# Phases of a gated recurrence as running sums of angles, with every step of the kernel in a new order

## The chip, the core and the metric

The kernel runs on one core of one Trainium2 chip. The core has five engines, each with its own in-order instruction queue: PE (TensorE, matrix products; its weight loads are listed as PEld), DVE (VectorE), ACT (ScalarE), POOL (GpSimd) and SP (SyncE, which here only issues DMAs). They synchronise through semaphores. Work waits for its inputs and for a free buffer, and everything queued behind a waiting instruction on the same engine waits too. The metric is the device time of one execution in microseconds; a kernel's time is the median of its runs.

## The reference

Inputs q, k, v, a_re, a_im have the shape (4, 8, 768, 48): batch, heads, tokens, channels. A complex gate per token and channel multiplies a state, then the rows of x go through a two-layer MLP.

```python
mag = np.sqrt(a_re * a_re + a_im * a_im)
scale = np.minimum(mag, 0.999) / (mag + 1e-06)
a_re_n, a_im_n = (a_re * scale, a_im * scale)
for t in range(S):
    ar, ai = (a_re_n[:, :, t, :, None], a_im_n[:, :, t, :, None])
    new_re = ar * S_re - ai * S_im
    new_im = ar * S_im + ai * S_re
    kv = np.einsum('bhd,bhe->bhde', k[:, :, t], v[:, :, t])
    S_re, S_im = (new_re + kv, new_im)
    y[:, :, t] = np.einsum('bhd,bhde->bhe', q[:, :, t], S_re)
...
h = x @ w_in
g = np.maximum(h, 0.0) + alpha * np.minimum(h, 0.0)
return (g @ w_out).astype(np.float32)
```

x is y with heads and channels side by side: 3072 tokens of 384. w_in is 384 x 2048, w_out 2048 x 384; both arrive as 64-bit floats.

A gate is a size times a rotation. So the state is real in a frame that turns: k and q are multiplied by the cosine and sine of the phase summed up so far, and only the sizes remain as decays.

## The kernel before, in words

**Units.** A unit is one chunk of 128 tokens of one batch, all 8 heads: 24 units, function `unit`. A unit turns q and k by the phases (L661, L663, tile PP), multiplies them by decays for block widths 1, 2, 4, 8, 16, 32 (`step`, L717; ACT copies at L740 and L756), forms products of queries and keys per block (`meet`, L678), masks them (L699 on ACT, L702 on DVE), transposes the keys (L785, L787), forms the new state (L797, L826, L829) and the result (L817, L841), which ACT copies out (L855) and two DMAs write to ysc (L860).

**Gates.** `gates` makes what the units load. It runs over nine groups, lettered A to I: batch 0 in groups of 1, 2 and 3 chunks, each other batch in two groups of 3. 384 head-channels lie as 3 x 128 rows, so a group of C chunks has N = 3 x 128 x C columns: 384, 768, and 1152 for a full group. The steps up to L310 normalise: ACT squares and takes reciprocal roots, DVE multiplies; `dec` holds the sizes, `x` and `y` the unit rotations. L318 multiplies sizes pairwise, level by level, and L323 writes them to the DRAM tensor decs, from which a unit loads T (L594). The phases are products of rotations: seven complex products within blocks of 8 tokens (`product`, L338 and L340), seven more over blocks of 64, one running chain over those (`run`, `carry`), a renormalisation (L405 to L413), and a last complex product per token (L426, L429). L431 writes cosine and sine to phs, from which a unit loads PP (L587). Operations of up to 80 elements go to POOL for batches 1 to 3 and to DVE for batch 0. The tile gate has two buffers, so group g's loads (L250) wait for group g - 2.

**Weights.** Sixteen pieces of 64-bit weights are loaded (L491) and converted to float32 by ACT (L507, L509, L511), POOL (L515) and DVE (L517, L519).

**MLP.** `features` multiplies a token group by one of 16 slices of w_in (L889, two PSUM buffers ps_h), ACT takes Relu (L896), DVE adds the rest (L898); `outputs` multiplies by w_out (L908), and L918 and L921 send it out. L873 loads x from ysc.

**The order.** Every piece of work is a Python generator; each `yield` ends a step that issues one to a few dozen instructions. The string ORDER names the generator that goes on next, a letter per step: A to I gates, J unit loads, K and L loads of v, M small loads and weights, N and O weight conversion, P to Z and a to m units 0 to 23, n the loads of x, o the MLP. The engines' queues are filled in this order and in no other; the numbers given to DVE(...), ACT(...) and the like at a yield are ignored here.

```python
for c in order:
    next(self.tasks[self.LETTERS.index(c)], None)
```

## Time and profile before

| what | value |
|---|---|
| median of 3 runs | 855.87 us (851.8 to 855.99) |
| span of the profiled execution | 853.8 us |
| mean granted TensorE clock | 0.958 |
| DMA traffic, mean | 130.91 MB, 153 GB/s |
| chain that ended last, by engine | PE 62%, DVE 17%, DMA 11%, issue 4%, ACT 3% |
| unit 0: first matmul, last result DMA | 50.6, 116.9 us |
| unit 3: first matmul, last result DMA | 173.6, 200.1 us |
| first load of x (L873) | 121.4 us |
| unit 23: last result DMA | 799.7 us |

A group of the profile's instruction list has its line, engine, operation, tiles written and read, shape and count, then busy time and the mean length of one in ns, then the idle time of its engine just before and what ended it. In the table of forty slices each digit is the busy share of 21 us in tenths. The sum of single durations on an engine can exceed its busy time a little, as neighbouring instructions overlap.

### The profile page before, as it was taken

How to read it: one execution, taken by the hardware profiler on the slowest of the kernel's cores; microseconds unless marked ns; L12 is line 12 of the kernel's file. 1: busy time of each engine (PE TensorE's matmuls, PEld its weight loads, DVE VectorE, ACT ScalarE, POOL GpSimd, SP SyncE). 2: the span in 40 equal slices, each digit the busy share in tenths (PEclk: the TensorE clock that was granted, in tenths of full speed). 3: DMA queues.
4: the chain of work that ended last, by engine and by line, in shares of the span. 5: the costliest groups of instructions: out<-in, count | busy, mean ns of one | idle time of the engine just before them, and what ended most of it. 6: DMA issues, size and time to landing. Idle time of an engine off the chain costs nothing.

```text
span 853.8 us, 26837 instructions
## 1 busy us (share of the span) xinstructions
PE 702.5 (82%) x11488; PEld 534.1 (63%) x11488; DVE 650.8 (76%) x1020; ACT 441.3 (52%) x937; POOL 203.3 (24%) x293
## 2 busy tenths in 40 slices
PE   0000428678999898999999799999999999999998
PEld 0000416557777676776677577777777777777776
DVE  5999989998998799778999686788896754643212
ACT  7848786565736444564567333456544333332211
POOL 6322142306526202440036400530006100000000
PEclk9999858689999999899999899999999999999999
DMA  6796784875398369747874479357654455421000
GB/s 202 235 245 211 219 226 137 246 188 142 98 275 182 77 159 242 187 112 182 222 202 105 129 195 206 96 144 192 151 174 100 135 132 133 108 51 35 20 28 10
DMA packets 194174, 130.91 MB, mean 153 GB/s; under 512 B 74120, under 2 KB 185864, under 8 KB 194056
## 3 DMA queue, kind: packets, MB, share of 16 engines
q1 hardware_dynamic: 194056, 129.20, 57.8%
q8 instruction: 90, 1.47, 0.7%
q14 instruction: 28, 0.23, 0.1%
HBM read 100.82 MB, written 35.71 MB: 160 GB/s over the span
## 4 chain that ended last, share of the span: by engine, by line
PE 62%; DVE 17%; DMA 11%; issue 4%; ACT 3%; SPq 2%; DVEq 0%; ACTq 0%
PE ps_o L908 24%; PE ps_h L889 23%; DVE KQ L717 4%; PE ps_lv L678 4%; PE ps_y L817 4%; DMA T<-decs 4%; PE ps_kv L797 3%; PE ps_y L841 2%; DVE gate L426 2%; PE ps_kt L785 2%; DMA PP<-phs 2%; DMA gate<-in_a_re_dram 1%; DVE gate L298 1%; DMA phs<-gate 1%; DVE gate L318 1%
## 5 line engine op out<-in xcount | busy, mean ns | idle before, releaser
L889 PE MATMUL ps_h<-xT,w_in_sb 128*128 128x256 f32 (+1 forms) x1344 | 305.3, 358 | 10.7 <-DMA xT<-ysc 8.2
L908 PE MATMUL ps_o<-w_out_sb,g_sb 128*128 128x384 f32 x768 | 293.8, 498 | 5.2 <-DVE g_sb L898 4.2
L889 PEld LDWEIGHTS ps_h<-xT,w_in_sb 128*128 128x128 f32 x1344 | 234.6, 194 | 82.9 <-DMA xT<-ysc 8.4
L898 DVE SCALAR_TENSOR_TENSOR g_sb<-g_sb,al,ps_h 128x256 f32<-128x256 f32 (+1 forms) x224 | 97.2, 436 | 116.9 <-ACT g_sb L896 116.5
L896 ACT ACTIVATE g_sb<-ps_h 128x256 f32<-128x256 f32 (+1 forms) x224 | 78.7, 352 | 204.3 <-PE ps_h L889 203.1
L717 DVE TENSOR_TENSOR KQ<-KQ,T 96x1024 f32<-96x1024 f32 x120 | 148.1, 1234 | 40.3 <-PE ps_lv L678 34.5
L908 PEld LDWEIGHTS ps_o<-w_out_sb,g_sb 128*128 128x128 f32 x768 | 139.4, 193 | 58.7 <-DVE g_sb L898 7.9
L678 PE MATMUL ps_lv<-WQ 96*32 96x32 f32 x2304 | 34.0, 202 | 78.7 <-DVE WQ L661 50.6
L678 PEld LDWEIGHTS ps_lv<-WQ 96*32 96x32 f32 x2304 | 26.1, 115 | 99.2 <-DVE WQ L661 50.6
L740 ACT COPY WQ<-KQ 96x1024 f32<-96x1024 f32 x48 | 50.0, 1042 | 27.0 <-DVE KQ L717 26.8
L515 POOL TENSOR_SCALAR top<-top 128x768 f32<-128x768 f32 x16 | 45.8, 2862 | 73.5 <-ACT top L507 62.8
L855 ACT COPY T<-ps_y 48x256 f32<-48x256 f32 x96 | 30.9, 364 | 51.6 <-PE ps_y L841 50.9
L817 PE MATMUL ps_y<-A,VL 64*48 64x64 f32 x2304 | 45.4, 232 | 14.4 <-issue 13.4
L338 POOL TENSOR_TENSOR gate<-gate 128x72 f32<-128x72 f32 x42 | 27.5, 654 | 118.1 <-ACT gate L368 115.3
L817 PEld LDWEIGHTS ps_y<-A,VL 64*48 64x48 f32 x2304 | 43.1, 133 | 15.4 <-issue 14.2
L338 DVE TENSOR_TENSOR gate<-gate 128x576 f32<-128x576 f32 (+5 forms) x84 | 47.9, 571 | 1.3
L699 ACT ACTIVATE A<-ps_lv,columns 128x64 f32<-128x64 f32 x144 | 36.9, 335 | 20.4 <-PE ps_lv L678 20.4
L756 ACT COPY W<-KQ 96x512 f32<-96x512 f32 x48 | 30.7, 639 | 30.0 <-DVE KQ L717 24.9
L426 DVE TENSOR_TENSOR gate<-gate 128x1152 f32<-128x1152 f32 (+2 forms) x36 | 43.4, 1231 | 2.1 <-POOL gate L411 2.0
L678 PE MATMUL ps_lv<-KQ,W 96*32 96x32 f32 x1536 | 24.3, 204 | 17.8 <-ACT W L756 15.8
L702 DVE TENSOR_TENSOR A<-ps_lv,mask 128x256 f32<-128x256 f32 x96 | 37.4, 411 | 0.0
L787 ACT COPY T<-ps_kt 128x384 f32<-128x384 f32 x48 | 23.1, 480 | 26.8 <-PE ps_kt L785 26.7
(106 smaller groups left out, 904.8 us busy)
## 6 DMA issues: line engine op xcount, KB each, us to landing
T<-decs SPq DMA_DIRECT2D x48, 384.0 KB
PP<-phs SPq DMA_DIRECT2D x24, 387.0 KB
KQ<-in_q_dram SPq DMA_DIRECT2D x48, 192.0 KB
decs<-gate SPq DMA_DIRECT2D x7, 1152.0 KB
phs<-gate SPq DMA_DIRECT2D x14, 576.0 KB
KQ<-in_k_dram SPq DMA_DIRECT2D x40, 192.0 KB
vsc<-in_v_dram SPq DMA_DIRECT2D x48, 144.0 KB
VL<-vsc SPq DMA_DIRECT2D x24, 288.0 KB
```

Source lines behind the costliest of these rows:

```text
L338: on(4 * k).tensor_tensor(out=m, in0=w[:, 1::-1].unsqueeze(2).to_broadcast([P, 2, 2, k]), in1=pairs_of(u), op=ALU.mult)
L426: TT(out=m[:, a], in0=U5[:, 1 + a], in1=turned(off3, o)[:, a].unsqueeze(1).unsqueeze(3).to_broadcast([P, L // 2, nb, 2]), op=ALU.mult)
L515: nc.gpsimd.tensor_scalar(out=top, in0=top, scalar1=F64_SMALL, scalar2=None, op0=ALU.max)
L678: nc.tensor.matmul(t[64 * i + j:64 * i + j + HC // 2, p], lhsT=keys(n, g), rhs=queries(n, g), start=True, stop=True)
L702: nc.vector.tensor_tensor(out=a.rearrange("p n (g t) -> p n g t", g=2), in0=t.unsqueeze(2).to_broadcast(whole), in1=masks[name].rearrange( ...
L717: nc.vector.tensor_tensor(out=x, in0=x if x0 is None else x0, in1=m, op=ALU.mult)
L740: nc.scalar.copy(z.rearrange("p i n t -> p i (n t)").rearrange("p i (m h) -> p m i h", h=h), bass.AP(tensor=KQ.tensor, offset=KQ.offset + ...
L817: nc.tensor.matmul(o, lhsT=Vp[h][64 * i:64 * i + 64, s, e_ * D:(e_ + 1) * D], rhs=a, start=False, stop=False)
L889: nc.tensor.matmul(p, lhsT=w_in_sb[:, f // 2, kk, f % 2 * P:(f % 2 + 1) * P], rhs=x_of[m][:, kk], start=(kk == 0), stop=(kk == NK - 1))
L896: nc.scalar.activation(gt, p, AF.Relu, scale=-1.0)
L898: nc.vector.scalar_tensor_tensor(out=gt, in0=gt, scalar=al_1[:, f:f + 1], in1=p, op0=ALU.mult, op1=ALU.add)
L908: nc.tensor.matmul(sums[0], lhsT=gt[:, c * P:(c + 1) * P], rhs=w_out_sb[:, f], start=(f == 0), stop=(f == NF - 1))
```

## The change

The gates are computed another way, and ORDER is a new string of 3791 letters (4292 before). Per group:

- An angle per token: ACT and DVE form a reciprocal of the real part (Abs_reciprocal_sqrt, two Squares, two products as a correction), the quotient of imaginary and real part, and its Arctan.
- The phase is the running sum of the angles, three `tensor_tensor_scan` of n tokens, begun with the phase of the group before (`carry`). It is brought into one turn: an Identity adds 1.5 x 2^23, the low 16 bits are the number of whole turns, and DVE subtracts them.
- Sine and cosine come from Sin, the cosine through the absolute value of the phase; two DMAs write them to phs, now with the first column.
- The size is the sum of real part times cosine and imaginary part times sine of the token's own angle. It is clipped, divided through and multiplied pairwise as before, then written to decs, now after phs.
- Two steps of the form `tensor_scalar` run on POOL, in group A on DVE. A Sin of one column stands ahead of each Arctan.
- The complex products, their tiles and their small DMAs are gone. A group has 42 steps (41 where it is a batch's last) in place of 91 to 100. The units, loads, weights and MLP have the same steps as before, issued in the new order.

```diff
 ORDER = (
-    "AAAAAAAAAMJBMMMMMAAAAAAAAAOAAAAAKAAAABAAAAAAAAAKAAKAKKKKKKKKKAAOAKBOKOBOBJAANBNAABBBNAAAOAAAAAANNAMA"
-    "AAAAKNANABNNAAAANBAAAAABJBBBANABMBMABAOAONJOABAAABBBBBMBAAAABAAOBAABAABBBBKOBBBBBBBBBNNNNNBBJNBBPBBN"
...
-    "oooooooooooooooooooooooooooooooooooooooooooooooooooooooooooooooooooooooooooooooooooooooooooo")
+    "MMAJMMAAAAAAAAAANAAAAAAMBJNAAAAANJJMAAAABKLAALAMLNBAKKAAAAAANNABBBBAAAABBBONOOBOOOOOBBONNJKKKAKPNNPP"
+    "BBMJCJJCNBBBBBNNOBNBBBBBPPPPPNNPOOPJMMLBLKJBJMLCBKBBBNPBCBBBCPOOCPBBBBBBOOCCCCPCPPPOOPNNNNMCNNCCONJQ"
...
+    "ooooooooooooooooooooooooooooooooooooooooooooooooooooooooooooooooooooooooooooooooooooooooooo")
...
-    bias_half = next(column)
-    nc.vector.memset(bias_half, -0.5)
+    bias_round = next(column)
+    nc.vector.memset(bias_round, 1.5 * 2.0 ** 23)
+    bias_back = next(column)
+    nc.vector.memset(bias_back, -TURN / 4)
+    bias_quarter = next(column)
+    nc.vector.memset(bias_quarter, TURN / 4)
+    ones, trig = next(column), next(column)
+    nc.vector.memset(ones, 1.0)
...
-        flat = work.tile([P, 6 * NK * GT], F32, tag="gate", name="gate", bufs=2)[:, 0:6 * N]
-        G = flat.rearrange("p (r n) -> p r n", r=6)
-        x, c, f, d, e, y = [G[:, i] for i in range(6)]
-        dec = flat[:, 3 * N:5 * N].rearrange("p (m s) -> p m s", s=TL)
-        for z, src in ((x, a_re), (y, a_im)):
-            z = z.rearrange("p (t s) -> p t s", t=NK)
+        flat = work.tile([P, 6 * NK * GT + 2 * NK], F32, tag="gate", name="gate", bufs=2)
+        x, c, d, e = [flat[:, i * N:(i + 1) * N] for i in range(4)]
+        dec = flat[:, 2 * N:4 * N].rearrange("p (m s) -> p m s", s=TL)
+        wide = [flat[:, 4 * N + i * NK * (n + 1):4 * N + (i + 1) * NK * (n + 1)] for i in range(2)]
+        turn, sine = [z.rearrange("p (t s) -> p t s", t=NK) for z in wide]
+        spun, y = turn[:, :, 1:n + 1], sine[:, :, 1:n + 1]
+        def rows3(z):
+            return z.rearrange("p (t s) -> p t s", t=NK)
+        for z, src in ((rows3(x), a_re), (y, a_im)):
             rows = src[b].rearrange("n i d s -> (n i d) s").rearrange("(t p) s -> p t s", p=P)
             t = yield DMA(N / 2, ("gates", g - 2))
             if last:
                 nc.gpsimd.memset(z[:, :, n - 1:n], 0.0)
             nc.sync.dma_start(z[:, :, 0:n - last], rows[:, :, c0 * P + 1:c1 * P + 1 - last])
+            if z is y:
+                ty = t
+            else:
+                tx = t
+        if g:
+            t = yield POOL(N, tx)
+        else:
+            t = yield DVE(N // 2, tx)
+        (nc.gpsimd if g else nc.vector).tensor_scalar(out=d, in0=x, scalar1=1.5, scalar2=TINY, op0=ALU.mult, op1=ALU.add)
         t = yield ACT(N, t)
-        nc.scalar.activation(x, x, AF.Identity, scale=1.5, bias=bias_tiny)
-        yield ACT(N)
-        nc.scalar.activation(c, x, AF.Square, scale=GATE_SCALE)
+        nc.scalar.activation(c, d, AF.Abs_reciprocal_sqrt, scale=GATE_SCALE)
         t = yield ACT(N, t)
-        nc.scalar.activation(d, y, AF.Square, scale=1.5 * GATE_SCALE)
+        nc.scalar.activation(c, c, AF.Square)
+        t = yield ACT(N, t)
+        nc.scalar.activation(c, c, AF.Square)
         t = yield DVE(N, t)
-        TT(out=c, in0=c, in1=d, op=ALU.add)
+        TT(out=c, in0=d, in1=c, op=ALU.mult)
+        t = yield DVE(N, t)
+        TT(out=d, in0=d, in1=c, op=ALU.mult)
+        t = yield DVE(N, t, ty)
+        STT(out=rows3(c), in0=y, scalar=1.5, in1=rows3(c), op0=ALU.mult, op1=ALU.mult)
+        t = yield DVE(N, t)
+        STT(out=d, in0=d, scalar=2.0 / GATE_SCALE ** 2, in1=c, op0=ALU.subtract, op1=ALU.mult)
+        yield ACT(1)
+        nc.scalar.activation(trig, bias_one, AF.Sin)
+        ta = yield ACT(N, t)
+        nc.scalar.activation(d, d, AF.Arctan, scale=-GATE_SCALE ** 4)
+        t = yield ACT(NK, *[("carry", g - 1)] * (not first))
+        if first:
+            nc.scalar.activation(turn[:, :, 0], ident[:, 0:NK], AF.Copy, scale=0.0)
+        else:
+            nc.scalar.copy(turn[:, :, 0], carry)
+        for i in range(NK):
+            t = yield DVE(2 * n, ta, t)
+            nc.vector.tensor_tensor_scan(out=turn[:, i, 1:n + 1], data0=ones.to_broadcast([P, n]), data1=d[:, i * n:(i + 1) * n],
+                                         initial=turn[:, i, 0:1], op0=ALU.mult, op1=ALU.add)
+        ts = yield ACT(N, ta)
+        nc.scalar.activation(c, d, AF.Sin, scale=-1.0)
+        tc_ = yield ACT(N, ta)
+        nc.scalar.activation(e, d, AF.Sin, bias=bias_back)
+        ts = yield DVE(N, ts)
+        TT(out=rows3(c), in0=y, in1=rows3(c), op=ALU.mult)
+        tc_ = yield DVE(N, tc_)
+        TT(out=e, in0=x, in1=e, op=ALU.mult)
+        tm = yield DVE(N, ts, tc_)
+        TT(out=c, in0=c, in1=e, op=ALU.add)
         t = yield ACT(N, t)
-        nc.scalar.activation(d, c, AF.Abs_reciprocal_sqrt)
+        nc.scalar.activation(rows3(d), spun, AF.Identity, scale=1.0 / TURN, bias=bias_round)
+        whole = d.bitcast(I16)[:, 0::2]
+        t = yield DVE(N, t)
+        STT(out=spun, in0=rows3(whole), scalar=-TURN, in1=spun, op0=ALU.mult, op1=ALU.add)
+        if not last:
+            done["carry", g] = yield ACT(NK, t)
+            nc.scalar.copy(carry, turn[:, :, n])
+        scr = dram.tile([H * D, C, TL], F32, tag="decs", name="decs")
+        phs = dram.tile([H * D, 2, n + 1], F32, tag="phs", name="phs")
+        def send(o, after):
+            used = yield DMA(N / 2, after)
+            nc.sync.dma_start(phs[:, o].rearrange("(t p) s -> p t s", p=P), (turn, sine)[o])
+            return used
+        ts = yield ACT(N, t, tm)
+        nc.scalar.activation(wide[1], wide[0], AF.Sin)
         t = yield ACT(N, t)
-        nc.scalar.activation(e, d, AF.Square)
-        te = yield ACT(N, t)
-        nc.scalar.activation(f, e, AF.Abs_reciprocal_sqrt)
-        t = yield DVE(N, te)
-        TT(out=e, in0=e, in1=c, op=ALU.mult)
-        t = yield DVE(N, t)
-        STT(out=d, in0=e, scalar=3.0, in1=d, op0=ALU.subtract, op1=ALU.mult)
-        tf = yield ACT(N)
-        nc.scalar.activation(f, f, AF.Square, scale=ONE / (1.5 * GATE_SCALE * MAG_EPS), bias=bias_one)
-        tf = yield ACT(N)
-        nc.scalar.activation(f, f, AF.Abs_reciprocal_sqrt)
-        tf = yield ACT(N)
-        nc.scalar.activation(f, f, AF.Identity, scale=ONE / 2.0, bias=bias_half)
-        ts = yield DVE(N, t)
-        TT(out=c, in0=c, in1=d, op=ALU.mult)
-        ts = yield ACT(N, ts)
-        nc.scalar.activation(c, c, AF.Copy, scale=1.0 / (1.5 * GATE_SCALE))
-        L = 8
-        nb = N // L
-        U5 = G[:, 0:3].rearrange("p r (m n i) -> p r m n i", m=L // 2, i=2)
-        def U3(j):
-            return U5[:, :, j // 2, :, j % 2]
-        def UT(j):
-            return U3(j)[:, 1:3]
-        def by_place(z):
-            return z.rearrange("p (n m i) -> p m n i", m=L // 2, i=2)
-        for p, w in ((x, -0.5), (y, -0.75)):
-            tx = yield DVE(N, t)
-            STT(out=p, in0=p, scalar=w * GATE_SCALE, in1=d, op0=ALU.mult, op1=ALU.mult)
-        t = yield DVE(N, ts, tf)
-        STT(out=dec[:, :, 0:P], in0=c.rearrange("p (m s) -> p m s", s=P), scalar=-2.0 * MAG_CAP,
-            in1=f.rearrange("p (m s) -> p m s", s=P), op0=ALU.max, op1=ALU.mult)
+        nc.scalar.activation(wide[0], wide[0], AF.Abs)
+        yield from send(1, ts)
+        t = yield ACT(N, t)
+        nc.scalar.activation(wide[0], wide[0], AF.Sin, scale=-1.0, bias=bias_quarter)
+        used = yield from send(0, t)
+        for u in range(b * NCH + c0, b * NCH + c1):
+            scr_of[u] = (scr, phs, u - b * NCH - c0)
+            done["PP", u] = used
+        t = yield ACT(N, tm)
+        nc.scalar.activation(x, c, AF.Abs)
+        if g:
+            tm = yield POOL(N, t)
+        else:
+            tm = yield DVE(N // 2, t)
+        (nc.gpsimd if g else nc.vector).tensor_scalar(out=c, in0=c, scalar1=-MAG_CAP, scalar2=MAG_CAP, op0=ALU.max, op1=ALU.min)
+        t = yield ACT(N, t)
+        nc.scalar.activation(x, x, AF.Square, scale=1.0 / MAG_EPS, bias=ones)
+        t = yield ACT(N, t)
+        nc.scalar.activation(x, x, AF.Abs_reciprocal_sqrt)
+        t = yield DVE(N, t, tm)
+        STT(out=dec[:, :, 0:P], in0=x.rearrange("p (m s) -> p m s", s=P), scalar=1.0,
+            in1=c.rearrange("p (m s) -> p m s", s=P), op0=ALU.subtract, op1=ALU.mult)
         yield POOL(2 * NK * C, t)
         nc.gpsimd.memset(dec[:, :, TL - 2:TL], 0.0)
-        for o, p in ((2, y), (1, x)):
-            tu = yield ACT(N, tx, t)
-            nc.scalar.copy(U5[:, o], by_place(p))
-        tu = yield ACT(N)
-        nc.scalar.activation(G[:, 0], G[:, 2], AF.Copy, scale=-1.0)
-        f = y
         at = 0
         while at < TL - 4:
             m = (TL - at) // 2
...
             pairs = dec[:, :, at:at + m].rearrange("p m (n s) -> p m n s", s=2)
             on(k).tensor_tensor(out=dec[:, :, at + m:at + m + m // 2], in0=pairs[:, :, :, 0], in1=pairs[:, :, :, 1], op=ALU.mult)
             at += m
-        scr = dram.tile([H * D, C, TL], F32, tag="decs", name="decs")
-        phs = dram.tile([H * D, 2, n + 1], F32, tag="phs", name="phs")
-        sent = t = yield DMA(N, t)
+        t = yield DMA(N, t)
         nc.sync.dma_start(scr.rearrange("(t p) c s -> p t (c s)", p=P),
                           dec.rearrange("p (t c) s -> p t (c s)", t=NK))
         for u in range(b * NCH + c0, b * NCH + c1):
-            scr_of[u] = (scr, phs, u - b * NCH - c0)
             done["T", u] = t
...
-        for j in range(1, L):
-            t = yield from product(UT(j), U3(j), UT(j - 1), f, nb, t)
...
-        begin = work.tile([P, 2, NK], F32, tag="begin", name="begin", bufs=1)
-        t = yield ACT(2 * NK)
-        nc.scalar.copy(begin, off.rearrange("p r (t k) -> p r t k", t=NK)[:, :, :, 0])
-        for o in range(2):
-            yield DMA(2, t)
-            nc.sync.dma_start(phs[:, o, 0:1].rearrange("(t p) s -> p t s", p=P), begin[:, o].unsqueeze(2))
-        m = G[:, 3:5].rearrange("p a (m n i) -> p a m n i", m=L // 2, i=2)
-        for o, p in enumerate((x, y)):
-            for a in range(2):
-                yield DVE(N, t, sent)
-                TT(out=m[:, a], in0=U5[:, 1 + a], in1=turned(off3, o)[:, a].unsqueeze(1).unsqueeze(3).to_broadcast(
-                    [P, L // 2, nb, 2]), op=ALU.mult)
-            ts = yield DVE(N)
-            TT(out=by_place(p), in0=m[:, 0], in1=m[:, 1], op=ALU.add)
-            used = yield DMA(N / 2, ts)
-            nc.sync.dma_start(phs[:, o, 1:n + 1].rearrange("(t p) s -> p t s", p=P), p.rearrange("p (t s) -> p t s", t=NK))
-        t = used
-        for u in range(b * NCH + c0, b * NCH + c1):
-            done["PP", u] = t
-        done["gates", g] = used
+        done["gates", g] = t
...
         slots.append(slot)
+        R["top"].put(t)
         return t
```

## The prediction

> **What bounds the kernel now.** I read the page's engine shares and slices first, then the busy time in two stretches, then the gate tile in the same stretches, then single rows.
>
> ```profile
> PE 702.5 (82%) x11488; PEld 534.1 (63%) x11488; DVE 650.8 (76%) x1020; ACT 441.3 (52%) x937; POOL 203.3 (24%) x293
> ...
> PE   0000428678999898999999799999999999999998
> ...
> DVE  5999989998998799778999686788896754643212
> ...
> DMA  6796784875398369747874479357654455421000
> ```
>
> DVE is full in the early slices and TensorE (PE) in the late ones, so the kernel has a front that feeds TensorE and a rest in which TensorE is the limit. I put the border at 200 us, where unit 3 issues its last result DMA (L860, at 200.1 us).
>
> ```profile
> 0.00:200.00 200.00, 73.84 (x1800) 60.48 (x1801) 181.55 (x350) 141.69 (x232) 64.55 (x68) 0.86 0.74 210
> 200.00:854.00 654.00, 628.64 (x9690) 473.66 (x9689) 469.30 (x671) 299.59 (x706) 138.73 (x226) 0.99 0.54 136
> ...
> 0.00:200.00 200.00, 103.92 (x213) 61.99 (x84) 9.11 (x23) 0.86 0.74 210
> 200.00:854.00 654.00, 141.14 (x153) 83.24 (x105) 133.98 (x211) 0.99 0.54 136
> ```
>
> The first two lines are the whole core: stretch, then PE, PE's weight loads, DVE, ACT, POOL, the granted clock, DMA share, GB/s. In the front TensorE works 73.8 of 200 us (126 idle) and DVE 181.6; afterwards TensorE idles only 653.8 - 628.6 = 25.2 us. The last two lines are only what touches the tile gate (DVE, ACT, POOL): 103.9 of DVE's 181.6 us in the front are gate work. So the front is worth 126 us of idle TensorE at most, the rest 25.
>
> **The price rows.** Shape by shape:
>
> ```profile
> L426 DVE TENSOR_TENSOR gate<-gate 128x1152 f32<-128x1152 f32 x28 | 37.7, 1368 | 2.1 <-POOL gate L411 2.0
> L338 DVE TENSOR_TENSOR gate<-gate 128x576 f32<-128x576 f32 x49 | 37.0, 756 | 0.6
> L298 DVE SCALAR_TENSOR_TENSOR gate<-gate 128x1152 f32<-128x1152 f32 x14 | 18.6, 1349 | 0.0
> L340 DVE TENSOR_TENSOR gate<-gate 128x288 f32<-128x288 f32 x49 | 22.3, 455 | 0.6
> L253 ACT ACTIVATE gate<-gate,columns 128x1152 f32<-128x1152 f32 x7 | 8.8, 1253 | 0.0
> L264 ACT ACTIVATE gate<-gate 128x1152 f32<-128x1152 f32 x7 | 8.1, 1164 | 0.1
> L515 POOL TENSOR_SCALAR top<-top 128x768 f32<-128x768 f32 x16 | 45.8, 2862 | 73.5 <-ACT top L507 62.8 <-DMA St<-in_v_dram 10.6
> L269 DVE TENSOR_TENSOR gate<-gate 128x384 f32<-128x384 f32 x1 | 0.6, 558 | 1.1 <-ACT gate L267 1.1
> ```
>
> **DVE, per full group (N = 1152).** Removed: seven full-width operations of the normalisation (L259, L269, L271, L279, L298 twice, L301; 1.35 each, 9.5), seven block products (0.756 + 0.455, 8.5) and six final products and sums (L426, L429; 8.2): 26.2 us. Added: nine full-width operations, 9 x 1.35 = 12.2, and three running sums of 384 elements. The trace has no running sum. Its floor is the 128x384 row, 0.56 us; its ceiling, if each element waits for the one before, twice that, 1.1. I take the ceiling, since each sum does depend on the last: 3.3. The net is 15.5 for 26.2. The decay products (L318) stay. Over all groups, 245 us of gate work on DVE becomes about 141 (nine full-width operations 99, 27 sums 27, L318 16), with sums at the floor 128.
>
> [...]
>
> **ACT.** Removed: thirteen full-width steps per group (126 us over the run) and small copies (27). Added: again thirteen full-width steps, nine without and four with a bias column, at the rows above 126 us, and some 5 us of tiny ones. New is that Abs_reciprocal_sqrt and the Sin and Arctan steps alternate. Before has two table loads:
>
> ```profile
> 5.79 0.51 ACT L257 ACTIVATE gate<-gate 128x384 f32<-128x384 f32 x1
> 6.31 1.28 ACT L262 ACT_TABLE_LOAD   x1
> 7.61 0.52 ACT L262 ACTIVATE gate<-gate 128x384 f32<-128x384 f32 x1
> ```
>
> A switch costs 7.61 - 6.30 = 1.3 us here, nothing more before or after it. Counting the function changes along the new ORDER gives 19 loads, 11 ahead of the same point in unit 3: 17 x 1.28 = 22 us more over the run. ACT in all: 441 + 22 + 131 - 153 = 441, no change.
>
> **POOL.** Removed: the products and sums of the small blocks (L338, L340, L396 to L411 and others), 128 us. Added: two 1.5x-and-clip operations per group, except group A, whose two are on DVE. By L515, 3.73 ns an element, they take 4.3 us; nearest below, the two-operation L409 at 128x144 takes 0.556, the same rate; if two operations count twice, 8.6. I take 4.3: 14 x 4.3 + 2 x 2.9 = 66. The weights' L515 now queues behind them, and DVE's L517 and L519 wait for L515. POOL's work ahead of unit 3 grows from 49 to 70 us of some 180, so this lies beside other work; uncovered it is one 4.3 us delay of a weight piece at a time.
>
> **DMA and SP.** The 18 tiny begin DMAs go; 129.2 MB stay. All SP steps are in a new order, phs ahead of decs. Counting letters up to unit 3's last L860: 181 issues and 41.8 MB before, 183 and 42.4 MB after.
>
> **The sum.** Up to that point ORDER has 909 letters before and 755 after. Both issue nearly the same TensorE work there (74 and 78 MLP matmul steps, four units), so what is left for TensorE is equal, and the change is worth the shift of this point plus what goes from the 25.2 us behind it. Ahead of it lie groups A, B, C whole, D up to its last full-width operation but one, E to its second product: on DVE 9.5 + 13.5 + 17.1 + 14.1 + 10.1 = 64 us in place of 104, so DVE 181.6 - 104 + 64 = 142. On ACT 60 of steps and 14 of loads in place of 62: 141.7 + 12 = 154. DMA: 42.4 MB. So DVE's lead is gone and three resources lie close together. Before moved 210 GB/s on average up to 200 us at a share of 0.74; its better windows are 265 (25 to 50 us, share 0.93) and 243 (75 to 100 us, 0.85). At 265 the point comes at 160 us, at 215 at 197. With DVE no longer holding back the releases of buffers I take 238 GB/s: 178 us, which leaves ACT 86% and DVE 80% busy. Gain 22.
>
> Behind the point DVE and ACT have more room: I take 5 of the 25.2 us, with 0 and 13 as bounds, since part of that idle time stands behind T and PP loads that the earlier gates bring forward. Profiled execution: 853.8 - 22 - 5 = 827. The median of the runs shown is 855.87, 2.1 above the span, so 829.
>
> **Rivals.**
> 1. *DVE's relief arrives whole.* With DVE at the same 91% share the point comes at 200.1 x 142 / 181.6 = 157 us, and half of the later idle goes: 853.8 - 43 - 12 = 799, median 801. For it: DVE is the fullest engine in every early slice. Against it: 42.4 MB in 157 us are 270 GB/s, above the best 25 us window.
> 2. *ACT becomes the front's limit.* Four hand-overs a group make ACT wait for DVE (Arctan, the rounding step, the wide Sin, Abs). At rows of the kind "ACT gate L366 <- DVE gate L340" (13.1 us in 7 waits) 1.9 us each, 19 of them ahead of unit 3: 154 + 36 = 190, so 853.8 - 10 = 844, median 846. Against it: the order puts other ACT work between them.
> 3. *Nothing comes of it.* The row has its two loads at the very start; if a switch in mid-stream costs it twice, 11 x 1.3 = 14 us join rival 2's 190, the point stays at about 204, and nothing is gained: 855. Against it: the lines above leave 0.02 us on either side of the load. [...]
> 4. *Slower: ACT's queue holds TensorE in the late stage.* ACT runs in order, and behind a gate's waiting Arctan or Sin stand L896 (the MLP's Relu), L740 and L756. TensorE has two ps_h buffers, and a group of six L889 records takes 1.29 us, so it rides out about 2.6 us of waiting. Six late groups with five waits each (POOL's clip joins) are 30; TensorE loses 30 x (W - 2.6). It decides from W = 2.6 + 27/30 = 3.5 us; at W = 4.1 it costs 45: 827 + 45 = 872, median 874. For it: single waits of 7.8 us occur (L366). Against it: their mean is 1.9. The worst form belongs here too: before shows Copy, Relu, Square, Abs and Sign all under one table; were they missing beside Sin, 44 stretches of Sin and Arctan would each cost two loads, some 69 more loads, 88 us on ACT.
>
> **Chances.** Forecast 0.53 (its own range 814 to 842), rival 1 0.12, rival 2 0.16, rival 3 0.07, rival 4 0.12. About 0.5% is what a measurement of this kernel can tell from no change. Faster by more than that: 0.53 + 0.12 + 0.16 = 0.81; same 0.07; slower 0.12. The range runs from rival 1 to just past rival 2, 801 to 853.
>
> **What would show it.** In the changed profile: DVE busy near 545 and ACT near 441 with 19 table loads; running sums of 384 near 1.1 us; POOL's new operations near 4.3; POOL busy near 140; the first matmul near 40 us in place of 50.6 (ahead of it DVE work falls from 53 to 28 us, ACT's from 44 to 38); unit 3's last L860 near 178; a DMA share above 0.8 up to there; TensorE busy still near 700, with 20 us of idle time behind the point. ACT above 95% busy in the front would show rival 2, TensorE idle behind the point of over 45 us rival 4. The forecast is wrong if unit 3 leaves later than 190 us, or if TensorE's own busy time moves by over 10 us.

## The result, and the profile after

The changed kernel takes 888.8 us (median of 4 runs, 885.0 to 892.8), the kernel before beside it 853.8: a ratio of 1.042, 95% interval 1.036 to 1.047. It is 35 us slower; the forecast was 829, 27 us faster than the runs of before shown then. The profiled execution has a span of 891.1 us, 37.3 above that of before.

The engine shares and slices on the profile's page of the changed kernel, with the granted TensorE clock:

```profile
PE 726.3 (82%) x11488; PEld 541.1 (61%) x11488; DVE 579.5 (65%) x797; ACT 445.6 (50%) x887; POOL 122.1 (14%) x99
...
PE   0002356779888898999998889999999999999998
...
DVE  3999894898649668577878368485755645454112
...
PEclk9999657889889989999999899999999999999999
DMA  9979847774946675864347763566535424332000
```

DVE (579.5 us busy, 650.8 before) and POOL (122.1, 203.3) have less to do and ACT about as much (445.6, 441.3), which is the direction of the forecast. TensorE, whose instructions are the same 11488, is busy 23.8 us longer. Behind the front four slices of its clock row stand at 8; in the kernel before it is two.

The two stretches, the whole core first (PE, weight loads, DVE, ACT, POOL, clock, DMA share, GB/s), then tile gate alone (DVE, ACT, POOL):

```profile
0.00:200.00 200.00, 75.30 (x1786) 59.98 (x1788) 160.44 (x211) 146.61 (x219) 75.19 (x60) 0.85 0.80 213
200.00:892.00 692.00, 651.03 (x9710) 481.08 (x9704) 419.11 (x586) 299.00 (x668) 46.94 (x39) 0.97 0.50 128
...
0.00:200.00 200.00, 69.14 (x75) 56.32 (x66) 18.96 (x15) 0.85 0.80 213
200.00:892.00 692.00, 76.00 (x71) 71.02 (x65) 46.62 (x36) 0.97 0.50 128
```

In the front DVE's gate work fell from 103.9 to 69.1 us, yet TensorE did 75.3 us of work there in place of 73.8: almost nothing of the relief arrived. Unit 3's last result DMA, the forecast's point, left at 202.8 us (200.1 before). Behind 200 us TensorE is busy 651.0 instead of 628.6, and its idle time there grew from 25.2 to 891.1 - 200 - 651.0 = 40.1. So the whole loss, 22.4 + 14.9 = 37.3 us, shows on TensorE behind the front.

The groups of the new gate steps, shape by shape (busy, mean ns of one, idle before):

```profile
L342 POOL TENSOR_SCALAR gate<-gate 128x1152 f32<-128x1152 f32 x7 | 32.8, 4685 | 311.2 <-ACT gate L337 311.2
...
L295 DVE TENSOR_TENSOR_SCAN gate<-columns,gate 128x384 f32<-128x384 f32 x21 | 20.8, 1016 | 0.4 <-ACT gate L292 0.4
L305 DVE TENSOR_TENSOR gate<-gate 128x1152 f32<-128x1152 f32 x7 | 13.0, 1856 | 0.0
...
L268 POOL TENSOR_SCALAR gate<-gate 128x1152 f32<-128x1152 f32 x7 | 11.0, 1572 | 65.1 <-DMA gate<-in_a_re_dram 43.5 <-DMA VL<-in_v_dram 16.7 <-DVE w_in_sb L449 4.7
...
L303 DVE TENSOR_TENSOR gate<-gate 128x1152 f32<-128x1152 f32 x7 | 9.5, 1350 | 4.8 <-ACT gate L298 4.8
...
L284 ACT ACT_TABLE_LOAD x7 | 9.0, 1283 | 0.1
```

Line numbers are the changed kernel's. L268 is the multiply and add on POOL, L342 the clip (a maximum and a minimum). The two are of one form and one shape, and the clip takes three times as long. L303 and L305 are the same DVE operation at the same shape too, yet L305 takes 1.86 us on average and L303 1.35. The order of events shows why. First DVE and POOL at 110 us (start, duration, instruction):

```profile
110.16 1.35 DVE L303 TENSOR_TENSOR gate<-gate 128x1152 f32<-128x1152 f32 x1
...
110.34 5.12 POOL L342 TENSOR_SCALAR gate<-gate 128x1152 f32<-128x1152 f32 x1 [2.12 <-ACT gate L337]
111.42 4.90 DVE L305 TENSOR_TENSOR gate<-gate 128x1152 f32<-128x1152 f32 x1
```

Then at 194 us:

```profile
193.75 4.87 POOL L342 TENSOR_SCALAR gate<-gate 128x1152 f32<-128x1152 f32 x1 [21.30 <-ACT gate L337]
...
194.59 0.42 DVE L633 TENSOR_TENSOR A<-ps_lv,mask 128x256 f32<-128x256 f32 x1
...
194.92 0.55 DVE L760 TENSOR_TENSOR St<-St,ps_kv 96x384 f32<-96x384 f32 x1
...
195.50 3.19 DVE L757 TENSOR_TENSOR St<-St,T 96x384 f32<-96x384 f32 x1
```

And at 336 us, with TensorE:

```profile
336.04 4.32 POOL L342 TENSOR_SCALAR gate<-gate 128x1152 f32<-128x1152 f32 x1 [4.74 <-ACT gate L337]
336.33 4.76 DVE L594 TENSOR_TENSOR KQ<-KQ,PP 96x1024 f32<-96x1024 f32 x1
...
341.02 0.47 DVE L829 SCALAR_TENSOR_TENSOR g_sb<-g_sb,al,ps_h 128x256 f32<-128x256 f32 x1
...
341.54 1.26 PE L820 MATMUL ps_h<-xT,w_in_sb 128*128 128x256 f32 x3 [2.31 <-DVE g_sb L829]
```

Beside each of the seven clips of 128x1152 one DVE operation with both inputs in SBUF doesn't come to its end while the clip runs: L305 needs 4.90 us for 1.35 of work, L594 4.76 for 1.22, L757 3.19 for 0.55, and each of the seven ends 0.1 to 0.9 us after the clip. Operations that began before the clip (L303 in the first excerpt, 1.35 us) or within 0.1 us of its start (one, L276 at 271.4 us, 1.34) have their usual length, and so have those that read PSUM (0.42 us for L633 and 0.55 for L760 beside the second clip). DVE shows nothing but a longer busy time. The third excerpt shows how this reaches TensorE: the MLP's L829 stands in DVE's queue behind L594, both ps_h buffers wait for it, and TensorE waits 2.31 us for L829. Over the run, DVE operations that lasted over 0.35 us more than the median of their form add up to 28.4 us beyond that median (18 operations); 22.0 of it are eight operations that lie beside a clip. Before it was 6.0 us (12).

The waits of TensorE behind 200 us (total, times, longest), the first two in the changed kernel and the last two before, show that this is not where most of its idle time lies:

```profile
PE ps_y L748 <- issue: 19.7, 8, 4.2
...
PE ps_h L820 <- DVE g_sb L829: 2.3, 1, 2.3
```

```profile
PE ps_y L817 <- issue: 9.3, 5, 4.0
...
PE ps_h L889 <- DVE g_sb L898: 1.1, 2, 0.6
```

L748 and L817 are the same short matmuls of a unit's result, and "issue" means that the profile names nothing they waited for. They make up 10.4 of the 14.9 us by which the idle time grew.

### The profile page after: what moved, and what is told of

Read it like the earlier page. It is cut to its first block, busy times and chain, and to the rows that moved or that the text cites. A ratio compares the mean times of both kernels' runs of the same rounds, so it can differ in the third digit from the quotient of the medians.

```text
span 891.1 us, 26364 instructions
## 1 busy us (share of the span) xinstructions
PE 726.3 (82%) x11488; PEld 541.1 (61%) x11488; DVE 579.5 (65%) x797; ACT 445.6 (50%) x887; POOL 122.1 (14%) x99
## 4 chain that ended last, share of the span: by engine, by line
PE 66%; DVE 13%; issue 7%; DMA 6%; ACT 5%; SPq 1%; POOL 1%; DVEq 0%; ACTq 0%; POOLq 0%
PE ps_h L820 25%; PE ps_o L839 25%; PE ps_lv L609 4%; PE ps_y L748 4%; DVE KQ L648 4%; PE ps_y L772 3%; PE ps_kv L728 3%; DMA T<-decs 3%; PE ps_kt L716 2%; DVE KQ L594 2%; DMA gate<-in_a_im_dram 1%; DVE gate L305 1%; POOL top L445 1%; DVE g_sb L829 1%; DVE gate L295 1%
## 5 line engine op out<-in xcount | busy, mean ns | idle before, releaser
L820 PE MATMUL ps_h<-xT,w_in_sb 128*128 128x256 f32 (+1 forms) x1344 | 311.8, 365 | 9.2 <-DMA xT<-ysc 6.7
L839 PE MATMUL ps_o<-w_out_sb,g_sb 128*128 128x384 f32 x768 | 304.6, 511 | 14.2 <-DVE g_sb L829 11.3
L820 PEld LDWEIGHTS ps_h<-xT,w_in_sb 128*128 128x128 f32 x1344 | 240.3, 198 | 85.9 <-DMA xT<-ysc 6.8
L829 DVE SCALAR_TENSOR_TENSOR g_sb<-g_sb,al,ps_h 128x256 f32<-128x256 f32 (+1 forms) x224 | 97.7, 438 | 179.8 <-ACT g_sb L827 179.3
L648 DVE TENSOR_TENSOR KQ<-KQ,T 96x1024 f32<-96x1024 f32 x120 | 148.6, 1238 | 80.3 <-PE ps_lv L609 66.5
L839 PEld LDWEIGHTS ps_o<-w_out_sb,g_sb 128*128 128x128 f32 x768 | 138.9, 195 | 68.0 <-DVE g_sb L829 14.5
L609 PE MATMUL ps_lv<-WQ 96*32 96x32 f32 x2304 | 35.4, 205 | 53.8 <-DVE WQ L592 33.1
L342 POOL TENSOR_SCALAR gate<-gate 128x1152 f32<-128x1152 f32 (+1 forms) x8 | 35.8, 4481 | 315.1 <-ACT gate L337 315.1
L609 PEld LDWEIGHTS ps_lv<-WQ 96*32 96x32 f32 x2304 | 27.1, 117 | 75.1 <-DVE WQ L592 33.1
L748 PE MATMUL ps_y<-A,VL 64*48 64x64 f32 x2304 | 45.4, 226 | 24.3 <-issue 24.3
L748 PEld LDWEIGHTS ps_y<-A,VL 64*48 64x48 f32 x2304 | 41.1, 126 | 27.6 <-issue 27.4
L445 POOL TENSOR_SCALAR top<-top 128x768 f32<-128x768 f32 x16 | 46.4, 2906 | 60.4 <-ACT top L437 60.4
L687 ACT COPY W<-KQ 96x512 f32<-96x512 f32 x48 | 30.6, 637 | 41.1 <-DVE KQ L648 28.1
L772 PE MATMUL ps_y<-KQ,St 96*48 96x64 f32 x768 | 32.6, 241 | 7.9 <-DVE St L760 4.0
L609 PEld LDWEIGHTS ps_lv<-KQ,W 96*32 96x32 f32 x1536 | 19.9, 116 | 30.6 <-ACT W L687 27.6
L633 DVE TENSOR_TENSOR A<-ps_lv,mask 128x256 f32<-128x256 f32 x96 | 37.5, 413 | 0.0
L716 PE MATMUL ps_kt<-ident,KQ 96*128 96x96 f32 x192 | 26.7, 266 | 12.2 <-DVE KQ L648 11.2
```

Source lines behind the costliest of these rows:

```text
L445: nc.gpsimd.tensor_scalar(out=top, in0=top, scalar1=F64_SMALL, scalar2=None, op0=ALU.max)
L609: nc.tensor.matmul(t[64 * i + j:64 * i + j + HC // 2, p], lhsT=keys(n, g), rhs=queries(n, g), start=True, stop=True)
L648: nc.vector.tensor_tensor(out=x, in0=x if x0 is None else x0, in1=m, op=ALU.mult)
L716: nc.tensor.transpose(t[:, p], KQ[:, 1, 4 * i + p], ident[:D2, :D2])
L748: nc.tensor.matmul(o, lhsT=Vp[h][64 * i:64 * i + 64, s, e_ * D:(e_ + 1) * D], rhs=a, start=False, stop=False)
L772: nc.tensor.matmul(Y[64 * (n % 2):64 * (n % 2) + D, n // 4, n // 2 % 2, HC * s:HC * (s + 1)], lhsT=before[:, n], rhs=KQ[:, 0, n, HC * s:HC ...
```

## The experiments

Fifteen more kernels ran. "Both on DVE" stands for the change with L268 and L342 moved to DVE. Each ratio is to runs of the kernel before that were taken beside it (medians 852.6 to 855.5 us).

| kernel | us | ratio to before, 95% interval |
|---|---|---|
| the change | 888.8 | 1.042 (1.036 to 1.047) |
| e1: both on DVE | 867.9 | 1.020 (1.013 to 1.027) |
| e7: only the clip on DVE | 867.6 | 1.017 (1.011 to 1.024) |
| e4: the change, no table switches | 880.7 | 1.037 (1.028 to 1.046) |
| e12: both on DVE, no table switches | 873.4 | 1.022 (1.016 to 1.027) |
| e8: both on DVE, fewer bytes | 869.8 | 1.019 (1.010 to 1.027) |
| e2: new gates spread over the old order | 949.7 | 1.113 (1.105 to 1.121) |
| e3: old gates pressed into the new order | 1063.0 | 1.247 (1.239 to 1.255) |
| e5: both on DVE, all steps ordered anew | 880.7 | 1.033 (1.028 to 1.038) |
| e6: the kernel before, all steps ordered anew | 898.1 | 1.054 (1.046 to 1.061) |
| e9: as e5, second search | 873.0 | 1.024 (1.017 to 1.031) |
| e10: as e6, second search | 910.2 | 1.067 (1.061 to 1.073) |
| e11: both on DVE, old order of all else | 846.9 | 0.989 (0.984 to 0.995) |
| e15: as e11, gate steps placed by another search | 843.0 | 0.986 (0.981 to 0.991) |
| e13: the change's gates, order of e11 | 851.4 | 0.998 (0.994 to 1.002) |
| e14: only the clip on DVE, order of e11 | 844.2 | 0.990 (0.985 to 0.994) |

### POOL's two operations (e1, e7)

```diff
-        if g:
-            tm = yield POOL(N, t)
-        else:
-            tm = yield DVE(N // 2, t)
-        (nc.gpsimd if g else nc.vector).tensor_scalar(out=c, in0=c, scalar1=-MAG_CAP, scalar2=MAG_CAP, op0=ALU.max, op1=ALU.min)
+        tm = yield DVE(N // 2, t)
+        nc.vector.tensor_scalar(out=c, in0=c, scalar1=-MAG_CAP, scalar2=MAG_CAP, op0=ALU.max, op1=ALU.min)
```

e7 has this edit, e1 has it for L268 as well.

> The changed kernel with its two tensor_scalar per group (L268, L342) on DVE in all groups instead of POOL in eight of nine; nothing else. Theory P (POOL's L342 of 4.9 us holds back any DVE instruction that starts beside it: DVE rows of 1.2 us last up to 4.9, some 26 us in sum): the stretched DVE rows vanish, DVE busy falls from 580 to about 560 although it takes on 16 x 0.7 us, and the time falls from 889 to 855-870. Theory O (the new order of the steps costs it, whatever the engines do in the gates): the stretched rows vanish as well, but the time stays at 880 or more. Theory T (19 table loads on ACT): 885 or more.

> The changed kernel with only the second tensor_scalar of a group (maximum and minimum with a bound, 4.9 us on POOL) on DVE; the first (multiply and add, 1.6 us) stays on POOL. If it is the maximum and minimum that holds DVE while it runs, nearly all of the 21 us come back: 866 to 873 us, and the stretched DVE operations fall from 28 us in sum to under 8. If any operation of that width on POOL does it, half: 876 to 884.

e1 gave 867.9 us, e7 867.6, as theory P said (855 to 870 for e1). The clip alone is worth 21 us in the change as it stands; that the multiply and add costs anything on POOL can't be seen. The stretched operations on DVE, by the same measure, fell to 4.7 and 7.9 us. In e1 DVE has more to do and less time in which it is busy (565.9 us against 579.5). This is 21 of the 35 us. The front hardly moved, though: unit 3's last result DMA of e1 leaves at 199.7 us.

### ScalarE's tables (e4, e12)

```diff
-        nc.scalar.activation(c, d, AF.Abs_reciprocal_sqrt, scale=GATE_SCALE)
+        nc.scalar.activation(c, d, AF.Sign, scale=GATE_SCALE)
...
-        nc.scalar.activation(d, d, AF.Arctan, scale=-GATE_SCALE ** 4)
+        nc.scalar.activation(d, d, AF.Arctan, scale=-0.5)
...
-        nc.scalar.activation(x, x, AF.Abs_reciprocal_sqrt)
+        nc.scalar.activation(x, x, AF.Sign)
```

In these two the gates are computed with Sign in place of the reciprocal root and with another scale in the Arctan, to rid ACT of the table loads between them; the gates then hold other numbers.

> The changed kernel without its two reciprocal roots: Abs_reciprocal_sqrt becomes Sign (L270, L346) and the scale of the Arctan becomes -0.5, so all of ACT's functions share one table set; all instructions, sizes and waits stay, the numbers differ. Theory T: 1 or 2 table loads in place of 19, and the time falls to 860-875. Theories O and P: 880 or more, as 23 us of ACT lie beside other work.

> The changed kernel with both tensor_scalars on DVE (867.9 us) and no change of ScalarE's function table: Abs_reciprocal_sqrt is replaced by Sign, and the arctan's scale set to -0.5, so that the values differ. If the 19 table loads (1.3 us each) are what is left of the loss beside POOL's operation: 853 to 858 us, level with the kernel before. If they cost half of what they did in the change (8 us there): 861 to 866. If ScalarE's time has cover: 866 to 870.

e4 took 880.7 us, 8 below the change, with intervals that overlap; e12 took 873.4, not below e1's 867.9. The loads are down from 19 to 2 in both (ACT has 870 instructions in place of 887). Whole core by stretch, first both of e12, then the front of e1:

```profile
0.00:200.00 200.00, 78.37 (x1841) 62.42 (x1841) 158.27 (x221) 136.71 (x217) 53.82 (x53) 0.86 0.81 214
200.00:868.00 668.00, 635.89 (x9648) 471.44 (x9648) 407.62 (x593) 285.37 (x654) 17.30 (x30) 0.99 0.52 132
...
0.00:200.00 200.00, 78.50 (x1804) 62.37 (x1805) 157.10 (x220) 147.78 (x224) 53.70 (x53) 0.85 0.81 214
```

ACT (fourth column) is 11 us emptier in the front than with the switches (147.8 in e1), and TensorE does the same 78.4 us of work there (78.5). The table loads are no cause that these runs can tell from nothing once the clip is gone.

e4 and e12 also say something on the clip. They differ only in whether L268 and L342 run on POOL or on DVE, and lie 7 us apart (880.7 and 873.4), where the change and e1 lie 21 apart. So the 21 us are no fixed price of the clip: they hold for the change's order with its table loads in place. Why the clip costs less without the loads isn't shown.

### The DMA engines (e8)

```diff
-                nc.sync.dma_start(raw, src[f])
+                nc.sync.dma_start(raw[:, 0:1], src[f][:, 0:1])
...
-        lo, hi = raw[:, :, :, 0], raw[:, :, :, 1]
+        lo, hi = [raw[:, 0:1, :, i].to_broadcast([P, raw.shape[1], raw.shape[2]]) for i in range(2)]
```

Both operations are on DVE here, and 7.3 of the 12.6 MB of weights aren't loaded; what is missing is filled from the rows that are, so the MLP's numbers are others.

> The changed kernel with both tensor_scalars on DVE (867.9 us) and 7.3 of the 12.6 MB of weights not loaded: one of three, or of two, rows of each piece comes in, and the others are made from it. If unit 3's result at 200 us is held by the DMA engines (41.8 MB ahead of it at some 214 GB/s), it leaves 25 to 35 us sooner, and the kernel takes 835 to 850 us. If the chains of waits between the engines hold it, it leaves under 10 us sooner, and the kernel takes 858 to 868.

Unit 3 left at 196.2 us, which is the second answer, and the kernel took 869.8 us, 2 above the range that goes with it. The window of the front:

```profile
0.00:200.00 200.00, 83.16 (x1884) 66.72 (x1884) 159.67 (x224) 149.09 (x227) 54.16 (x53) 0.86 0.68 178
```

The DMA share fell from 0.81 to 0.68, and neither the point nor the end moved by more than 4 us, though TensorE did 83.2 us of work in this front, 4.7 more than in e1. With DVE at 80%, ACT at 75% and DMA at 68% no resource is full in the front. That leaves the chain of waits through the fixed order as what sets it; this is inferred from the three not being full, not shown wait by wait.

### The order: first, crude crossings (e2, e3)

```diff
 ORDER = (
-    "MMAJMMAAAAAAAAAANAAAAAAMBJNAAAAANJJMAAAABKLAALAMLNBAKKAAAAAANNABBBBAAAABBBONOOBOOOOOBBONNJKKKAKPNNPP"
-    "BBMJCJJCNBBBBBNNOBNBBBBBPPPPPNNPOOPJMMLBLKJBJMLCBKBBBNPBCBBBCPOOCPBBBBBBOOCCCCPCPPPOOPNNNNMCNNCCONJQ"
...
+    "AAAAAMJMMMMMAAAAOAAAKAAAAAAKAKAKKKKKKKKKAOAKOKOOJANNANAOAAANNAMAAKNANBNNAANAAABJBNABMMBAOONJOAABBBMB"
+    "AOBBBBKOBBBBNNNNNBBJNBPBNOBBJJOJOOONBBPPBPLBLLOBPBBBLLKLLNNNJPPPBBBLPBBBPPBLLLLMPOBMBPPPBMBLKLNKNKOK"
...
```

e2 has the string of before, with the letters A to I of the new gates spread evenly over the slots of the old ones. e3 has the kernel before's gates in the change's string, pressed into the first 29 slots of each group's gate steps.

> The changed kernel's gates in the order of before: every letter that is no gate stays where it was, and the 42 steps of a group are spread evenly over the places of its 91 to 100 old ones, from a tenth to nine tenths of them (group A from the start); still 19 table loads. Theory O: the cheaper gates now show their gain, 825-845. Theory P: POOL still holds DVE back, 860-890. Theory T: 860-885.

> The gates of before in the new order: every other letter stays where the change put it; the 91 to 100 old steps of a group go to the first 29 of its new places, three or four to a place, since phs has to be written by then. Theory O: 885 or more, the old gates being dearer too. Theory P and theory T: near before, 850-870, since neither L342 nor the extra table loads are there.

They took 949.7 and 1063.0 us, and e3's output holds other numbers than the reference's. Gate steps at bad places cost far more than anything the change does, so a crude crossing can't tell gates and order apart. What they show is the size of what is at stake in the string.

### The order: all steps searched anew (e5, e6, e9, e10)

For these a replay model was used: every step with its duration from the traces, the semaphore waits, a DMA speed and landing time. A search moved letters of the string. Nothing but ORDER is changed against e1 (e5, e9) and against the kernel before (e6, e10).

> The changed kernel with both tensor_scalars on DVE (867.9 us) and a third order of its steps, searched with a replay model that has the step durations, the DMA speed and the landing times of the traces (that model gives 856 for the kernel before, 863 for this kernel in the change's order, 818 in the new one). If the rest of the loss is the order alone: 820 to 848 us, below the kernel before. If the gates themselves, or transfers that no order can hide, keep unit 3's result at 200 us: 858 to 875 us.

> The kernel before with an order searched by the same model for as long (model 817 instead of 856). The control for the run above: if the two kernels' gates are worth the same once both are ordered alike, the two come within 8 us of each other; if running sums of angles are worth the 22 us that the prediction gave them, this one is 15 us or more above the other; if they cost time whatever the order, it is below it.

> The changed kernel with both tensor_scalars on DVE, again with a new order, searched by a replay model that now also prices each change of TensorE between a unit's short matmuls and the MLP's (0.15 and 0.20 us) and some stalls of 1 to 3.5 us; the order has 205 such changes where the change's has 291, the kernel before 243 and the order of the run that took 880.7 us 333. If those changes are what the new orders cost: 835 to 858 us, at or below the kernel before. If they are not, and any order made by a model loses what the model does not see: 865 to 885 us.

> The control: the kernel before with an order from the same search (215 changes instead of 243; the first such search gave 365 changes and 898.1 us). If the changes between short matmuls and the MLP's set what an order costs: 840 to 865 us, and with equal care for the order the running sums of angles come out 5 to 20 us ahead. If not: 870 to 895 us.

880.7, 898.1, 873.0 and 910.2 us: none came out below the kernel that it started from. For the first pair the model had promised gains of 45 and 39 us (863 to 818, 856 to 817); it leaves out something that decides. The theory behind the second pair, that the number of changes between short matmuls and the MLP's decides, fell: 215 changes instead of 243 made the kernel before 57 us slower. Two things can be read from them. Searched alike, the new gates come out ahead of the old ones (880.7 against 898.1, 873.0 against 910.2), so the new gates as such are not the loss. And e5 brings unit 3 at 177 us, the time that the forecast asked for, and is slow all the same: TensorE has issued 38 MLP steps by then, where before, change and e1 have 75 or 76. The unit came early at the MLP's cost.

### The order of before, with only the gates placed anew (e11, e15)

All letters J to Z, a to o in the sequence of the kernel before; the search may move only A to I.

> The changed kernel with both tensor_scalars on DVE, in an order in which every step outside the gate groups stands where the kernel before has it, word for word, and only the new gate steps are placed between them by the replay model (which puts it 9 us below the kernel before; the evenly spread gates of the first such run took 949.7 us). If the 1.4 to 2% that are left with both tensor_scalars on DVE come from the new order of units, loads and MLP: 840 to 858 us. If they come from what the new gates themselves need: 865 us or more.

> Both tensor_scalars on DVE, all other steps in the order of the kernel before, and the gate steps placed by the same search from another start (the replay model has it 3.6 us above the first). If what makes the run of 846.9 us fast is the order of the units, loads and MLP that it shares with the kernel before: 843 to 856 us. If it was the lucky place of single gate steps: 858 to 875.

846.9 and 843.0 us: below the kernel before, with two different placements of the gate steps. The windows of e15, whole core:

```profile
0.00:200.00 200.00, 85.17 (x2037) 68.89 (x2040) 154.38 (x226) 142.58 (x226) 47.18 (x53) 0.97 0.80 216
200.00:842.00 642.00, 617.18 (x9476) 463.24 (x9461) 409.68 (x589) 303.81 (x664) 9.11 (x30) 0.99 0.55 136
```

TensorE does 85.2 us of work in the front (73.8 before, 75.3 in the change, 78.5 in e1) and idles 841.9 - 200 - 617.2 = 24.7 us behind it. Here the relief of DVE arrives. The higher clock of this front (0.97) isn't the reason: in e11 it is 0.88, near the 0.86 of before, and TensorE does 83.2 us of work.

The same units by their times, read from each trace:

| us | before | change | e1 | e5 | e11 | e15 | e13 |
|---|---|---|---|---|---|---|---|
| unit 0: first matmul | 50.6 | 33.1 | 32.4 | 28.1 | 48.8 | 51.1 | 48.3 |
| unit 3: last result DMA | 200.1 | 202.8 | 199.7 | 177.0 | 187.4 | 185.3 | 190.3 |
| unit 12: last result DMA | 462.2 | 486.3 | 472.8 | 428.0 | 451.5 | 456.0 | 460.1 |
| unit 23: last result DMA | 799.7 | 851.9 | 826.0 | 842.7 | 785.8 | 788.0 | 796.8 |
| span | 853.8 | 891.1 | 865.2 | 881.1 | 839.7 | 841.9 | 850.8 |

e11's 12.7 us at unit 3 are 13.9 at unit 23 and 14.1 at the end: with the rest of the order kept, what the front gains stays. These are single executions, and e11's is the fastest of its four; by the medians the gain at the end is 8.5 us (855.5 to 846.9), and 9.8 in e15 (852.8 to 843.0).

The rest of the order is not all that counts, though. e2 keeps it as well, and with the change's gates only spread evenly it took 949.7 us; e13 below has the same instructions and the same sequence of all other letters, and takes 98 us less through the places of the gate letters alone.

### POOL's clip in the order of before (e13, e14)

e13 is the change with nothing but ORDER replaced by that of e11; e14 has the clip on DVE besides.

> The change's gate groups exactly as they are (both tensor_scalars of a group on POOL), in the order of the run that took 846.9 us: every other step stands as in the kernel before. If POOL's maximum and minimum costs what it cost in the change's order (21 us): 862 to 873 us, slower than the kernel before. If it costs that much only because the change's order has no slack behind it: 845 to 856.

> The same order with only the maximum and minimum on DVE and the multiply and add on POOL. If the hold on DVE is the maximum and minimum's alone: 843 to 851 us, level with the 846.9 us of both on DVE. If every POOL operation of that width holds DVE: 853 to 862.

e13 took 851.4 us, no different from the kernel before; e14 844.2. Here the clip costs 7 us, not 21. The hold on DVE is there all the same (e13, near 407 us):

```profile
407.46 4.28 POOL L342 TENSOR_SCALAR gate<-gate 128x1152 f32<-128x1152 f32 x1 [50.46 <-ACT gate L337]
...
407.83 4.64 DVE L594 TENSOR_TENSOR KQ<-KQ,PP 96x1024 f32<-96x1024 f32 x1
...
412.92 0.48 PE L820 MATMUL ps_h<-xT,w_in_sb 128*128 128x256 f32 x1 [2.77 <-DVE g_sb L829]
```

The stretched operations of e13 add up to 19.5 us, and TensorE waits for L829 as in the change, but unit 3 is 10 us earlier than in the kernel before. Most of that lead is gone at the end (unit 23 is 2.9 us ahead). With the clip on DVE it stays: e14's unit 3 leaves at 188.3 us and its unit 23 at 786.8, 11.8 and 12.9 ahead.

So the 37 us between the change and e13 (888.8 and 851.4) are the string alone: both have the same instructions and 19 table loads, in other places. The granted clock doesn't explain them: one execution of the change at a mean clock of 0.973 took 886.7 us, and one of e13 at 0.960 took 853.5.

## Why the prediction was wrong

**What held.** The gates' work on DVE and ACT. A running sum of 384 took 1.016 us on average where the ceiling of 1.1 was taken; that ceiling, twice the row of 0.56, was the author's estimate, as the kernel before has no running sum. DVE's gate work came to 145.1 us (141 said), ACT to 445.6 us with 19 table loads (441 and 19 said). A switch in mid-stream runs from 111.54 to 112.86 us, 1.32 in all (1.3 said). The first matmul moved forward, and by more than was said (33.1 us, near 40 said).

**The step that failed first: the border as the measure.** The prediction said that up to unit 3 both orders issue nearly the same TensorE work, so that the change is worth the shift of this point, and it put the point at 178 us because DVE's 142, ACT's 154 and the DMA rate at 238 GB/s would allow it. It stayed at 202.8, at 213 GB/s. None of the three resources held it, taken one at a time: e8 took DMA away, e12 took ACT time away, DVE was relieved by the change itself, and in the change's order the point stayed between 196 and 203 us in all of them (202.8, 199.7 in e1, 198.5 in e12, 196.2 in e8). So the sum of busy times was a floor for the front, and the kernel didn't come down to it. In the order of before the same gates (both tensor_scalars on DVE) moved the point to 185 to 187 us, 13 to 15 of the 22 us forecast, and the end by 8.5 to 9.8 us in the medians where 27 were forecast. The prediction counted the letters of the new order and put their effect at nothing; it was 37 us (the change against e13), more than the gates gained anywhere.

**The second: POOL's term "lies beside other work".** POOL was priced at 66 us added and hidden. It was less, 47.6 us (L268 took 1.57 instead of 4.3 us, the clip 4.69), but the clip isn't beside DVE's work: it stops it. DVE came to 579.5 us instead of 545, and 22.4 of those 34 us are the growth of stretched operations, 28.4 - 6.0. In the change that cost 21 us at the end (e1, e7), without its table loads 7 (e4, e12), and in the order of before 7 (e13, e14). Held beside the clips of 128x1152 were operations with both inputs in SBUF (L305, L594, L648, L757, by 2.3 to 3.6 us), not L633, L760 or L829, which read PSUM. How long a hold lasts is not the same for every operation of POOL: beside L445, the weights' maximum of 2.9 us, no DVE operation that began while it ran grew by more than 0.63 us, and beside L268, of 1.57 us, by no more than 0.94. By what means POOL holds DVE is not shown.

**The third: TensorE's 700 us and 20 us of idle time behind the point.** It was 726.3 and 40.1 us. In e11, e13 and e15 TensorE is busy 697 to 702 us, so the growth doesn't come with the gates; in the change's order it is 714.4 without the clip (e1) and 712.8 with the clip but no table switches (e4). A part of it is the granted clock: behind 200 us it stands at half for 41.0 us in the change, for 17.9 before, for none in e11. TensorE was busy for 38.4 of these 41.0 us, for 16.1 of the 17.9. A matmul of L839 took 849 ns at half clock and 497 at full on average, so an estimate from these rows is 22.3 x (1 - 497 / 849) = 9 of the 22.4 us. But the change's execution with the highest mean clock (0.973) took 886.7 us, no less than the 885.0 of one at 0.952, so a higher clock alone brought no time back. What sets the clock is not shown; one such stretch (342.0 to 345.4 us) begins 0.5 us after the wait for L829 in the third excerpt.

The idle time went another way than the prediction had it: 5 of 25.2 us were to go because T and PP loads come earlier. Instead the waits of "issue" at L748 grew from 9.3 to 19.7 us. They are 17.1 to 19.8 us in the kernels with the change's order, clip or not (e1, e4, e7, e12), and 4.7 to 6.7 in e11, e13, e14 and e15, so they go with the order; but waits of "issue" at other lines are longer in these, and all of them together come to 20.5 us in the change and 14.3 in e13.

**The rivals.** DVE's relief whole and ACT as the front's limit are out: ACT is busy 147 of 200 us. Table switches at double price, which rival 3 supposed and no run shows, are out by the trace (1.32 us for one in mid-stream) and by e12. Rival 4, slower through a queue that holds TensorE in the late stage, had the right direction and the wrong engine. TensorE does run out of ps_h buffers behind a held queue (2.31 us in the third excerpt), but the queue is DVE's, and what holds it is POOL, not a wait of ACT: e13 keeps every hand-over of ACT and all 19 loads and loses nothing against the kernel before. Nor did its sign show: TensorE idled 40.1 us behind the point, not over 45. That the time lies nearest to this rival's 874 is luck. No rival had the order itself as a cost.

**What stays open.** Which places in the change's string cost the 21 to 25 us between e1 and e11 or e15 isn't settled, nor whether it is those of the gate letters or of the others: the change's sequence of all else with the gate letters placed anew was not run. In the traces most of it is TensorE being busy for longer with the same matmuls: of the 25.5 us between the spans of e1 and e11, 17.1 (714.4 and 697.3 us busy). Ruled out as the sole cause are DMA bytes, table loads and the number of changes between a unit's short matmuls and the MLP's (291 in the change, 243 before, 205 in e9, which took 873 us).

## What to carry to other kernels

Where the order of all steps is written out, new steps and a new order are two changes: put the new steps into the old order first, with care for their places, and measure that. A string is worth tens of microseconds here (37 between two of them with the same instructions, 98 between two that differ only in the places of the gate steps), and the kernel before in a string searched on a model was 44 us slower where the model promised 39 less. Before work is moved to POOL as free, look at what DVE does beside it: a clip of 128x1152 there held DVE operations with two SBUF inputs for up to 3.6 us each, and moving it to DVE brought 7 to 21 us. Such a price is not the same in every surrounding, so one pair of runs doesn't fix it. A point in the front that comes sooner is worth something only if the same work of the engine that sets the end has been done by then.

## What was not expected of the hardware

- On POOL a tensor_scalar of multiply and add on 128x1152 took 1.57 us on average, one of maximum and minimum 4.69; the shortest of each took 1.15 and 4.08. The price of an element from one pair of operations did not carry over to the other.
- TensorE had waits of up to 4.2 us in the middle of a run of short matmuls (L748) for which the page of the profile names no releaser ("issue", 24.3 us ahead of that group in the whole run of the change, 13.4 before, 6.8 in e15). In four of the change's eight over 1 us a fetch of 16 KB by the instruction queue begins inside the gap (one at 309.3 us, in a gap from 308.1 to 311.8). That the fetch is the cause was not tried.
- With 7.3 of 12.6 MB of weights not loaded, and 178 instead of 214 GB/s in the front, the time of the change's order with both operations on DVE stayed as it was (869.8 us, 867.9 in e1).
